# An opening in 128-token pieces, a first tile loaded by two queues, and GpSimd's setup moved behind the second set of loads

## The chip, the cores and the metric

The kernel runs on one core of a Trainium2 chip. The metric is device time in microseconds (us) of one launch, from many executions; each is listed with the clock that the throttle granted to TensorE. The profiled span is about 1.8 us shorter than the time of the same execution, so spans are compared with spans and times with times. Engine names: PE is TensorE, DVE is VectorE, ACT is ScalarE, POOL is GpSimd, SP is SyncE.

## The reference

Two layers of the same kind over 2048 tokens of width 1024 in bf16. Each layer has a dilated local attention (8 keys, 2 apart) and a token-mixing MLP (3584 wide).

```python
def _A_ref(x, wqkv, wo):                       # attention, 32 heads of 32
    qkv = (x @ wqkv).reshape(B, S, 3, H, Dh) ...
    idx = pos[:, None] - (arange(8) * 2)[None, :]       # keys s, s-2, ..., s-14
    logits = einsum("bhsd,bhswd->bhsw", q, k[idx]) * scale;  logits[idx < 0] = -1e9
    return einsum("bhsw,bhswd->bhsd", softmax(logits), v[idx]) ... @ wo
def _B_ref(x, w1, b1, w2, b2):                 # MLP over the tokens
    h = layernorm(x); u = gelu(einsum("bsd,sf->bdf", h, w1) + b1)
    return (einsum("bdf,fs->bds", u, w2) + b2).transpose(0, 2, 1)
x = A_x                                        # twice:
x = x + _A_ref(layernorm(x), wqkv, wo);  x = x + _B_ref(layernorm(x), w1, b1, w2, b2)
```

Since keys are 2 apart, even and odd tokens never meet in the attention. The kernel calls them class 0 and class 1 and works on 8 tiles of 128 tokens of each.

## The kernel before

Its opening loads the 8 tiles of class 0, normalizes and transposes them on the fly, and projects q, k and v. The tiles of class 1 are loaded into the same buffers as these come free, all eight by GpSimd's queue in order:

```python
def staged(c, i):
    n = (i + c * (NT - 1)) % NT          # class-1 tile 0 -> buffer 7, tile 1 -> buffer 0, ...
    return g[n // GF][:, n % GF, :]

def x_stage(c, i):
    eng = nc.gpsimd if c else (nc.scalar if i % 2 else nc.sync)
    eng.dma_start(out=staged(c, i), in_=xin_v[c, i])
# ... in first_tiles (8 tiles of class 0):
idle(16); moments(0); own_sum(0); moments(1); norm(0); turn(0); idle(3)
own_sum(1); moments(2); norm(1); turn(1); idle(5); place(0, act); ...
for u, i in (((1, 0), 2), ((1, 1), 3), ((0, 0), None)):      # first projections, 256 columns
    banks[u] = bank(); project(*u, 0, banks[u], 0, 2 * P)
# ... (cut)
for u in ((1, 0), (1, 1), (0, 0), (0, 1)):                   # the "second half"
    project(*u, 1, bank(), 0, HT)
# ... opening():
for i in range(NT): x_stage(0, i)
load_biases()
first_tiles(hT, partial(at_.project, 0))
for i in range(NT): x_stage(1, i)
```

`moments` are layer-norm statistics on DVE (BATCH_NORM_STATS2) with the root on ACT, `norm` normalizes, `turn` transposes on TensorE, `place` copies the transpose out of PSUM, `idle` are dummy products that keep TensorE clocked up. Class-1 tiles are handled by two engines in turn, and scores are a DVE product `T` that TensorE then sums over the head:

```python
def prologue_tile(c, i, hT):              # class 1
    t = staged(c, i)
    if i % 2: nm, rs = stats_act(t, ...);  norm_act(t, t, nm, rs)      # odd tiles on ACT
    else:     mean, rs = stats_dve(t, ...); norm_dve(t, t, mean, rs)   # even tiles on DVE
    to_hT(t, hT, c, i)                    # DMA transpose
# scores, for each pair of heads' group and parity:
T = q (broadcast) * window(k)             # DVE, 128x4096
sc += sel^T @ T                           # TensorE, 8 products of 512 columns; needs T
```

`sel` and `maskc` are constants that GpSimd writes with some forty small fills. q and k reach DVE through casts on ACT, which stand in ACT's program order between the statistics of class-1 tiles 1, 3, 5 and 7.

Of the kernel before, what the change touches and what calls it, by code (L numbers as in the profile page):

```python
# [15 lines left out]
P = 128  # L16
H = 32
DH = 32
# [4 lines left out]
NEG = -1e9  # L23
# [3 lines left out]
def kernel(  # L27
# [13 lines left out]
    nc = tc.nc  # L41
# [7 lines left out]
    NT = SC // P  # L49
    HT = SC // 2  # L50
    NDC = D // 512
    HD = P // DH
    DQ = 4
# [56 lines left out]
    def bank(name="ps"):  # L110
        return psp.tile([P, 512], FP32, name=name, tag="ps")
# [10 lines left out]
    def st(name, shape):  # L122
        return stat.tile(shape, FP32, name=name, tag=name)
# [13 lines left out]
    slots = wins[0] + wins[1]  # L137

    sel = const.tile([P, SB * DQ, 32], BF16, name="sel")
    nc.gpsimd.memset(sel[:], 0.0)  # L140
    for sb in range(SB):
        for dq in range(DQ):
            for hp in range(HD):
                col = sb * CH + dq * HD + hp
                nc.gpsimd.memset(sel[hp * DH:(hp + 1) * DH, sb * DQ + dq, col:col + 1], 1.0)
    maskc = const.tile([P, W, W], FP32, name="maskc")
    nc.gpsimd.memset(maskc[0:CH], 0.0)
    for s, w in enumerate(slots):
        if w:
            nc.gpsimd.memset(maskc[0:CH, s, 0:w], NEG)  # L150
    b1_bf = const.tile([P, FT], BF16, name="b1_bf")
    b2_bf = const.tile([P, NT, DIL], BF16, name="b2_bf")
    b1_sb = const.tile([P, FT], FP32, name="b1_sb")
    b2_sb = const.tile([P, NT, DIL], FP32, name="b2_sb")

    def load_biases():
        with nc.allow_non_contiguous_dma(reason="tiny bias loads"):
# [39 lines left out]
    def rsqrt(dst, var, mul, eps):  # L197

        ln = st("ln", [P, 1])
        nc.scalar.activation(out=ln[:], in_=var, func=ACT.Ln, bias=eps[:], scale=mul)  # L200
        nc.scalar.activation(out=dst, in_=ln[:], func=ACT.Exp, scale=-0.5)
# [33 lines left out]
    def norm_act(dst, x, nm, rs):  # L235
        bi = st("bi", [P, 1])
        nc.scalar.activation(out=bi[:], in_=nm[:], func=ACT.Identity, scale=rs[:])
        nc.scalar.activation(out=dst, in_=x, func=ACT.Identity, bias=bi[:], scale=rs[:])  # L238
# [4 lines left out]
    def staged(c, i):  # L243
        n = (i + c * (NT - 1)) % NT
        return g[n // GF][:, n % GF, :]

    def x_stage(c, i):
        eng = nc.gpsimd if c else (nc.scalar if i % 2 else nc.sync)
        eng.dma_start(out=staged(c, i), in_=xin_v[c, i])

    def first_tiles(hT, project):
        tiles = [staged(0, i) for i in range(NT)]
        mv, rs, tps = {}, {}, {}
        s1, t1, nm, ss = (st(n, [P, w]) for n, w in (("s1", NDC), ("t1", 1), ("nm", 1), ("ss", 1)))
        junk = x2("junk")
        own = NT // 2

        def idle(n):
            ps = bank()
            for _ in range(n):  # L260
                nc.tensor.matmul(ps[:].rearrange("p (b t) -> p b t", t=P), lhsT=ident[:],
                                 rhs=ident[:].unsqueeze(1).to_broadcast([P, 4, P]), start=True, stop=True)

        def moments(i):
            s = st("bn", [P, NDC, 6])
            for n in range(NDC):
                nc.vector.bn_stats(out=s[:, n, :], in_=tiles[i][:, n * 512:(n + 1) * 512])
            mv[i] = st("mv", [P, 2])
            nc.vector.bn_aggr(out=mv[i][:], in_=s[:])
            rs[i] = st("rs", [P, 1])  # L270
            rsqrt(rs[i][:], mv[i][:, 1:2], 1.0, eps1)

        def norm(i):
            norm_dve(tiles[i], tiles[i], mv[i][:, 0:1], rs[i])

        def own_sum(n):
            nc.scalar.activation(out=junk[:, n * 512:(n + 1) * 512], in_=tiles[own][:, n * 512:(n + 1) * 512],
                                 func=ACT.Identity, accum_out=s1[:, n:n + 1])

        def own_square():  # L280
            nc.scalar.activation(out=t1[:], in_=s1[:, 1:2], func=ACT.Copy, scale=-1.0 / D)
            nc.scalar.activation(out=nm[:], in_=s1[:, 0:1], func=ACT.Identity, bias=t1[:], scale=-1.0 / D)
            nc.scalar.activation(out=junk[:], in_=tiles[own], func=ACT.Square, bias=nm[:], accum_out=ss[:])
            rs[own] = st("rs", [P, 1])
            rsqrt(rs[own][:], ss[:], 1.0 / D, eps1)

        def turn(i):
            tps[i] = psp.tile([P, KD, P], BF16, name="tp", tag="ps")
            for kt in range(KD):
                nc.tensor.transpose(tps[i][:, kt, :], tiles[i][:, kt * P:(kt + 1) * P], ident[:])  # L290

        def place(i, copy):
            copy(out=hT[0][i // 4][:, :, (i % 4) * P:(i % 4 + 1) * P], in_=tps.pop(i)[:])

        dve, act = nc.vector.tensor_copy, nc.scalar.copy
        idle(16)
        moments(0)
        own_sum(0)
        moments(1)
        norm(0)  # L300
        turn(0)
        idle(3)
        own_sum(1)
        moments(2)
        norm(1)
        turn(1)
        idle(5)
        place(0, act)
        moments(3)
        place(1, dve)  # L310
        norm(2)
        norm(3)
        banks = {}
        for u, i in (((1, 0), 2), ((1, 1), 3), ((0, 0), None)):
            banks[u] = bank()
            project(*u, 0, banks[u], 0, 2 * P)
            if i:
                turn(i)
        own_square()
        place(2, act)  # L320
        place(3, dve)
        norm_act(tiles[own], tiles[own], nm, rs[own])
        moments(own + 1)
        moments(own + 2)
        for n, u in enumerate(banks):
            project(*u, 0, banks[u], 2 * P, HT)
            if n == 0:
                turn(own)
                norm(own + 1)
                place(own, dve)  # L330
                moments(own + 3)
                norm(own + 2)
        for n, u in enumerate(((0, 1), (1, 2), (1, 3))):
            if n == 2:
                norm(own + 3)
            turn(own + 1 + n)
            place(own + 1 + n, dve)
            project(*u, 0, bank(), 0, HT)
        for u in ((1, 0), (1, 1), (0, 0), (0, 1)):
            project(*u, 1, bank(), 0, HT)  # L340

# [519 lines left out]
    for li in range(2):  # L861
# [7 lines left out]
                nc.gpsimd.memset(t[:, :, 0:PADK + 2], 0.0)  # L869

        def opening():
            for i in range(NT):
                x_stage(0, i)
            load_biases()
            clear_pads()
            with tc.manual_schedule(engines={getattr(mybir.EngineType, e) for e in ("PE", "DVE", "Activation", "Pool")}):
                first_tiles(hT, partial(at_.project, 0))
                for i in range(NT):
                    x_stage(1, i)
            yield "at", 27.0, 29.0  # L880
            for u in ((1, 2, 1), (1, 3, 1), (0, 2, 0),):
                yield from at_.proj(0, *u)
# [75 lines left out]
```

## Time and profile before

| before | |
|---|---|
| time, median of 3 runs at first, of 6 beside the changed kernel | 1280.26 us; 1280.51 us (1280.16 to 1280.95) |
| profiled span, granted clock | 1278.8 us, 1.00 |
| first statistics, first projection, second half | 4.63, 11.98, 25.61 us |
| class-1 loads issued by GpSimd | 24.35 to 28.64 us |
| first T on DVE; waits of TensorE before the first two score products | 35.05 us; 0 and 1.24 us |

The lines that carry the reading are in the prediction. One more view: DVE's timeline between the opening and the first T (start, length, engine, line, operation, output and inputs, count, and in brackets the idle time before it and what ended that; line numbers are those of the kernel that ran).

```profile
27.47 1.29 DVE L207 BATCH_NORM_STATS2 bn<-gg 128x6 f32<-128x512 bf16 x2 [2.69 <-DMA gg<-in_A_x_dram]
30.34 1.29 DVE L207 BATCH_NORM_STATS2 bn<-gg 128x6 f32<-128x512 bf16 x2 [1.34 <-DMA gg<-in_A_x_dram]
32.13 1.28 DVE L207 BATCH_NORM_STATS2 bn<-gg 128x6 f32<-128x512 bf16 x2 [0.26 <-DMA gg<-in_A_x_dram]
33.34 0.53 DVE L233 TENSOR_SCALAR gg<-gg,mv,rs 128x1024 bf16<-128x1024 bf16 x1
```

DVE waits for class-1 tiles 0, 2 and 4 one after the other as they land, and reaches T 2.92 us after the last of these (35.05 - 32.13).

### The profile page before, as it was taken

The numbers are of one execution on the slowest core, as the hardware profiler recorded it, in microseconds if no ns is written. First come the engines' busy times: TensorE is split into PE (matmuls) and PEld (weight loads), VectorE is DVE, ScalarE is ACT, GpSimd is POOL, SyncE is SP. The second block draws the span as 40 slices with busy tenths as digits, with TensorE's granted clock in tenths as the row PEclk, the third lists the DMA queues.
The fourth block names the chain that finished last, engine by engine and source line by source line (L and its number), as shares of the span: only waits on it lengthen the run. The fifth ranks groups of instructions, "written<-read, shape, count | busy, mean of one in ns | idle before, by whom it ended". The sixth has DMA issues, their size and how long they took to land.

```text
span 1278.8 us, 15455 instructions
## 1 busy us (share of the span) xinstructions
PE 1258.0 (98%) x6163; PEld 577.4 (45%) x6284; DVE 689.9 (54%) x869; ACT 489.3 (38%) x812; POOL 61.3 (5%) x166
## 2 busy tenths in 40 slices
PE   8999999999999999999999999999999999999998
PEld 4344444444444444444444444444444444444444
DVE  6789999999114322334798834899930233111011
ACT  6845446634424533324533445453352343000000
POOL 3000000001000000000000000010010000000000
PEclk9999999999999999999999999999999999999999
DMA  9853454553422289952738542358262223344331
GB/s 256 190 124 106 99 139 142 171 143 115 132 83 83 64 220 305 291 161 87 187 103 201 152 124 80 83 159 207 66 181 83 82 67 89 107 128 135 99 115 52
DMA packets 217817, 173.00 MB, mean 135 GB/s; under 512 B 32081, under 2 KB 198353, under 8 KB 215697
## 3 DMA queue, kind: packets, MB, share of 16 engines
q1 hardware_dynamic: 206768, 126.11, 36.5%
q0 software_dynamic: 9248, 37.51, 10.5%
q10 hardware_dynamic: 1728, 8.39, 1.7%
q8 instruction: 49, 0.80, 0.3%
q14 instruction: 24, 0.19, 0.0%
HBM read 139.47 MB, written 26.21 MB: 130 GB/s over the span
## 4 chain that ended last, share of the span: by engine, by line
PE 76%; DVE 5%; issue 2%; ACT 1%; DMA 0%; DVEq 0%
PE ps L719 30%; PE ps L743 29%; PE ps L418 11%; PE ps L664 4%; DVE T L456 2%; PE sc L480 1%; DVE pr L538 1%; DVE pr L543 1%; DVE xr L689 0%; ACT h L227 0%; ACT h L238 0%; DMA wo<-in_A_wo_dram 0%; DVE v L545 0%; DVE xr L692 0%; ACT ln L200 0%
## 5 line engine op out<-in xcount | busy, mean ns | idle before, releaser
L719 PE MATMUL ps<-h,w 128*128 128x512 bf16 x1754 | 385.6, 379 | 4.0 <-ACT h L238 2.0
L743 PEld LDWEIGHTS <-w 128*128 128x128 bf16 x1820 | 177.6, 98 | 209.9 <-issue 2.1
L719 PEld LDWEIGHTS <-w 128*128 128x128 bf16 x1792 | 175.2, 98 | 214.1 <-issue 3.4
L418 PE MATMUL ps<-hT,wq 128*128 128x512 bf16 (+1 forms) x1087 | 240.2, 374 | 2.5 <-issue 0.6
L743 PE MATMUL ps<-g,w 128*128 128x512 bf16 (+1 forms) x1017 | 225.9, 376 | 1.2 <-issue 0.2
L743 PE MATMUL ps<-gg,w 128*128 128x512 bf16 (+1 forms) x766 | 170.9, 376 | 0.9 <-issue 0.2
L418 PEld LDWEIGHTS <-wq 128*128 128x128 bf16 x1112 | 109.1, 100 | 128.8 <-issue 9.1
L748 DVE SCALAR_TENSOR_TENSOR xr<-ps,b_sb,xr 128x512 bf16<-128x512 f32 (+1 forms) x65 | 45.5, 738 | 225.1 <-PE ps L743 182.6
L456 DVE TENSOR_TENSOR T<-q,k 128x4096 bf16<-128x4096 bf16 x44 | 99.0, 2284 | 70.5 <-ACT q L422 52.4
L543 DVE TENSOR_TENSOR pr<-pr 128x2048 bf16<-128x2048 bf16 (+1 forms) x128 | 119.4, 949 | 0.3
L730 DVE TENSOR_TENSOR tmp<-ps,gg 128x512 f32<-128x512 f32 x48 | 33.2, 692 | 150.2 <-PE ps L719 148.2
L418 PE MATMUL ps<-hT,wv 128*128 128x512 bf16 x436 | 99.5, 380 | 0.6
L664 PE MATMUL ps<-wo,oT 128*128 128x512 bf16 x377 | 88.6, 379 | 1.1 <-DVE oT L545 0.7
L425 ACT CAST k<-ps 128x1024 bf16<-128x1024 f32 x60 | 60.7, 1014 | 61.0 <-PE ps L418 59.0
L538 DVE TENSOR_TENSOR pr<-pb,v 128x2048 bf16<-128x2048 bf16 x64 | 75.9, 1218 | 10.8 <-ACT v L425 6.1
L538 DVE TENSOR_TENSOR pr<-pb,g 128x2048 bf16<-128x2048 bf16 x64 | 76.6, 1216 | 7.6 <-DMA pb<-pd 5.1
L418 PEld LDWEIGHTS <-wv 128*128 128x128 bf16 x448 | 48.9, 111 | 48.7 <-issue 4.2
L730 DVE TENSOR_TENSOR tmp<-ps,g 128x512 f32<-128x512 f32 x48 | 33.2, 692 | 49.7 <-PE ps L719 46.9
L664 PEld LDWEIGHTS <-oT 128*128 128x128 bf16 x384 | 37.3, 98 | 46.8 <-issue 1.2
L422 ACT CAST q<-ps 128x512 bf16<-128x512 f32 x60 | 34.9, 586 | 49.5 <-PE ps L418 49.5
L731 ACT ACTIVATE gg<-tmp,b_sb 128x512 bf16<-128x512 f32 x48 | 34.6, 721 | 49.9 <-DVE tmp L730 49.9
L731 ACT ACTIVATE g<-tmp,b_sb 128x512 bf16<-128x512 f32 x48 | 34.6, 721 | 43.5 <-DVE tmp L730 43.1
(97 smaller groups left out, 755.9 us busy)
## 6 DMA issues: line engine op xcount, KB each, us to landing
w<-in_B_w_dram SPq DMA_DIRECT2D x56, 512.0 KB, 4.8
w<-in_B_w_dram SPq DMA_DIRECT2D x64, 448.0 KB, 3.8
wq<-in_A_wqkv_dram SPq DMA_DIRECT2D x38, 512.0 KB, 4.3
pb<-pd POOLq DMA_DIRECT2D x16, 1024.0 KB, 8.7
wo<-in_A_wo_dram SPq DMA_DIRECT2D x16, 512.0 KB, 3.9
xa<-xr POOLq DMA_DIRECT2D x32, 256.0 KB, 3.4
xr<-xa SPq DMA_DIRECT2D x32, 256.0 KB, 4.0
wv<-in_A_wqkv_dram SPq DMA_DIRECT2D x14, 512.0 KB, 5.4
```

The costliest lines, as they stand in the source:

```text
L418: nc.tensor.matmul(ps[:, lo:hi], lhsT=cols, rhs=self.hT[c][hf][:, kt, lo:hi], start=(kt == 0), stop=(kt == KD - 1))
L422: nc.scalar.copy(out=self.q_of(c, dt)[:, hf * HT:(hf + 1) * HT], in_=ps[:])
L425: nc.scalar.copy(out=window(buf, 0, PADK + hf * HT, [(KW + 1, 2), (1, HT)]), in_=ps[:].unsqueeze(1).to_broadcast([P, 2, HT]))
L456: mult = nc.vector.tensor_tensor(out=T, in0=q.unsqueeze(1).to_broadcast([P, 4, SC]), in1=window(k, par, 2, [(2, 4), (1, SC)]), op=ALU.mult)
L538: mult = nc.vector.tensor_tensor(out=pr[:, :, u, :], in0=pb[:, :, u, :], in1=window(self.v_of(c, dt), par, 2 + hf * HT, [(TB, 4), (2, 4), ...
L543: nc.vector.tensor_tensor(out=pr[:, :, 0:wd, :], in0=pr[:, :, 0:wd, :], in1=pr[:, :, wd:2 * wd, :], op=ALU.add)
L664: nc.tensor.matmul(banks[(i, n)][:], lhsT=at_.oT[c][kt][:, i * P:(i + 1) * P], rhs=wo_t[n][kt // 4][:, kt % 4, :], start=(kt == 0), stop=( ...
L719: nc.tensor.matmul(ps[:], lhsT=wt[c][:, i, fl * P:(fl + 1) * P], rhs=h2[c][i // 4][:, i % 4, dc * 512:(dc + 1) * 512], start=(k == 0), sto ...
L730: nc.vector.tensor_tensor(out=tmp[:], in0=ps[:], in1=gs, op=ALU.add)
L731: nc.scalar.activation(out=gs, in_=tmp[:], func=ACT.Gelu_apprx_tanh, bias=b1_sb[:, ft:ft + 1])
L743: nc.tensor.matmul(ps[:, 0:xc.stop - xc.start], lhsT=w2t(ft, c), rhs=g[ft // GF][:, ft % GF, xc], start=(ft == 0), stop=(ft == FT - 1))
L748: nc.vector.scalar_tensor_tensor(out=xo[:, xc], in0=ps[:, 0:xc.stop - xc.start], scalar=b2_sb[:, i, c:c + 1], in1=xo[:, xc], op0=ALU.add, ...
```

## The change

The intent: put the first tile at the head of both queues, interleave statistics so that tile 0 is normalized sooner, start projecting with 128 columns as soon as one tile is transposed, and clear GpSimd's queue and the DMA engines of setup work in the first microseconds.

```diff
+    def constants():                      # sel and maskc: formerly at the start, as straight code
+        nc.gpsimd.memset(sel[:], 0.0); ...
-        idle(16); moments(0); own_sum(0); moments(1); norm(0); turn(0); ...
+        idle(14)
+        stats(0, 0); stats(0, 1); root(0); stats(1, 0); norm(0); turn(0); stats(1, 1); root(1)
+        place(0, act); own_sum(0); idle(3); stats(2, 0); norm(1); turn(1)
+        for u in ((1, 0), (1, 1)):
+            project(*u, 0, banks[u], 0, P)             # 128 columns
         ... (order of the other tiles cut; second half unchanged)
         def opening():
-            for i in range(NT): x_stage(0, i)
-            load_biases()
+            x_stage(nc.sync, 0, 0, slice(0, P // 2))
+            x_stage(nc.scalar, 0, 0, slice(P // 2, P))
+            x_stage(nc.scalar, 0, 1)
+            x_stage(nc.sync, 0, 2); at_.weights(0, 1, 0); x_stage(nc.scalar, 0, 3); ...
             first_tiles(...)
             for i in range(NT):
                 x_stage(nc.gpsimd, 1, i)
+            constants()
+            load_biases()
```

## The prediction

> **What bounds the kernel now.** I read the page first, then busy time by stretch, then the timeline of the first 50 us. The page says that TensorE is busy for nearly the whole span:
>
> ```profile
> span 1278.8 us, 15455 instructions
> PE 1258.0 (98%) x6163; PEld 577.4 (45%) x6284; DVE 689.9 (54%) x869; ACT 489.3 (38%) x812; POOL 61.3 (5%) x166
> ```
>
> So 20.8 us of TensorE idle time (1278.8 - 1258.0) is all there is to win, besides work that counts as busy and is not needed. The stretches (start:end, length, then busy us of PE, PEld, DVE, ACT, POOL, then clock, DMA share, GB/s) tell where it lies:
>
> ```profile
> 0.00:12.00 12.00, 8.28 (x41) 3.46 (x42) 7.32 (x18) 5.52 (x16) 7.57 (x61) 1.00 0.92 265
> 12.00:25.60 13.60, 13.45 (x119) 9.38 (x121) 9.46 (x19) 9.63 (x19) 1.65 (x5) 1.00 1.09 230
> 25.60:32.60 7.00, 6.95 (x33) 3.21 (x33) 3.46 (x7) 5.15 (x13) 3.04 (x6) 1.00 0.94 299
> 32.60:40.00 7.40, 6.16 (x41) 2.51 (x39) 7.40 (x11) 7.40 (x21) 0.00 (x0) 1.00 0.83 184
> ```
>
> From 12 us on TensorE is full, with one hole in the fourth row. Before 12 us it is idle for 3.7 us, and most of its 8.28 busy us is the dummy products (16 + 3 + 5) that only keep it clocked up. The timeline shows what ends this phase (start, length, engine, line, operation):
>
> ```profile
> 1.57 5.30 PE L261 MATMUL ps<-ident 128*128 128x512 bf16 x16 [1.57 <-POOL ident masks.py:199]
> 4.63 1.29 DVE L267 BATCH_NORM_STATS2 bn<-gg 128x6 f32<-128x512 bf16 x2 [3.73 <-DMA gg<-in_A_x_dram]
> 7.47 0.54 DVE L233 TENSOR_SCALAR gg<-gg,mv,rs 128x1024 bf16<-128x1024 bf16 x1
> 8.06 0.62 PE L290 MATMUL tp<-ident,gg 128*128 128x128 bf16 x8 [1.19 <-DVE gg L233]
> 9.35 0.49 DVE L233 TENSOR_SCALAR gg<-gg,mv,rs 128x1024 bf16<-128x1024 bf16 x1
> 11.20 0.64 DVE L293 COPY hT<-tp 128x1024 bf16<-128x1024 bf16 x1
> 11.98 1.03 PE L418 MATMUL ps<-hT,wq 128*128 128x256 bf16 x8 [0.38 <-ACT t L281]
> 25.61 7.07 PE L418 MATMUL ps<-hT,wq 128*128 128x512 bf16 x31
> ```
>
> Tile 0 lands at 4.63, is normalized at 7.47, transposed at 8.06; the first projection has 256 columns, so it needs tiles 0 and 1, and starts at 11.98, just after the copy of tile 1 ends (11.20 + 0.64 = 11.84). The named releaser, a small ACT instruction, is a coincidence: the program has no such dependence. From 11.98 TensorE runs without a break to the second half (25.61) and to 32.6. **The opening is a chain load, statistics, root, normalize, transpose, copy, and the rest of the kernel is TensorE work behind it.**
>
> **What the Trainium skill says.** "DMA: Bandwidth & Descriptors", Rules for kernel authors: splitting a transfer into partition halves, or over SP and ACT, buys no bandwidth, since both share the same 16 DMA engines. The trace agrees: tiles 0 and 1, issued at 0.74 (SP) and 0.77 (ACT), landed 3.9 and 4.0 us later, together. So the split of tile 0 can help only by putting it alone at the head of both queues. The same section: a strided last dimension becomes one descriptor per element. The bias loads are such (3,584 + 2,048 two-byte elements); between 12 and 16 us, before they land, the DMA engines are mostly busy yet move 77 GB/s on average, against 335 to 385 from 4 to 10 us. "TensorE: Matmul & The Clock Gate", part 1: the array starts at half clock and needs some 3.4 us of activity; the weight loads of the dummies are 0.43 us apart up to 4.96 and 0.2 after, so the clock is up by about 5 us.
>
> **The change, part by part.** Writing t0 for the landing of tile 0, with durations from the timeline.
>
> *Loads.* The bytes moved by 3.9 us (sum of the GB/s slices) are about 0.51 MB, the size of two tiles, and both had landed 0.7 us later. Alone at the head, 0.26 MB is moved by about 3.15; adding the same 0.7 gives t0 = 3.85, a gain of 0.8 us (estimate). Key weights went fifth on SP (issued 2.61, landed 10.9); now they go third, behind about 1.3 MB in all, so they land near 7 (estimate), well before they are needed. Tiles 5 to 7 move back to about 9.5 to 11 and are needed from 12.
>
> *DVE order.* Before, all of tile 1's statistics stood between tile 0's and its normalization (start to start 7.47 - 4.63 = 2.84). Now only one half does: two halves of 0.64, aggregate 0.13, half of tile 1 under ACT's two root steps (0.77 from the aggregate's start), gives 2.12. Gain 0.7 us.
>
> *Pieces.* Following all engines in program order from t0: tile 0 normalized 2.12, transposed 2.7; its copy on ACT stands behind the root of tile 1 and runs 3.9 to 4.9; tile 1 normalized 4.0, transposed 4.6 to 5.2. The first 128-column products start at t0 + 5.2 = 9.0, not 11.98. They add little: eight transposes, of the same width, step through in 0.45 us, so two pieces cost 0.9 as does the 256-column group (0.9 to 0.95 by its spacing). Then, from t0: two pieces to 6.1; wait for tile 2's transpose, 6.5; two second pieces to 7.85; query group 8.8; transpose 9.2; second query group 10.1; four 256-column groups with two transposes to 14.7; a 512-column group (1.72) 16.4; transpose, 256 columns, transpose, 256 columns to 19.1. ACT is close behind (the tile it normalizes itself is ready at 12.4, wanted at 12.9), and the last copy (19.0) just precedes the second half. **The second half starts at t0 + 19.1 = 22.95, not 25.61: 2.66 us earlier**, of which 0.8 from the load and the rest from order and pieces. Seven dummies fewer cost nothing: they filled waits.
>
> *GpSimd.* The identity comes no later: six pad fills take the place of the large fill of 0.32 us. Its constants (about 5 us) now follow the class-1 loads. Those wait for the last transpose, so they move from 24.35 to about 22.4 and are issued by 26.7; constants end near 32. Their first reader, the score product, was at 37.80 and will come near 35: 3 us to spare. The bias loads then meet the class-1 transposes and cost DMA a slow stretch like that of 12 to 16 us, but near 32 to 37. Biases themselves are not read for hundreds of us.
>
> *What follows.* Products after the second half run on without waits to the first score product. The hole there is its second half, waiting for DVE:
>
> ```profile
> 35.05 2.27 DVE L456 TENSOR_TENSOR T<-q,k 128x4096 bf16<-128x4096 bf16 x1
> 39.65 0.61 PE L480 MATMUL sc<-T,sel 128*32 128x512 bf16 x8 [1.24 <-DVE T L456]
> ```
>
> DVE came to it late because class-1 tiles landed late (idle until 27.5, 30.3, 32.1). They now have DMA nearly to themselves, so I expect DVE near 31.7 instead of 35.05, and the hole to shrink from 1.24 to about 0.7. Sum: 2.66 + 0.5 = 3.2 us at 40 us. I take off 0.5 for parts of the later schedule that DVE sets (95.1 of 100 us busy from 100 to 200) and for DMA delays: **2.7 us, 1277.6 us, 0.2%.**
>
> **Rivals.** (a) *Nothing is gained*: the attention stage has DVE at 95%, so a head start on TensorE is given back as waits for DVE. Against: TensorE idles only 1.2 of 100 us there, and DVE starts earlier too. It would leave 1280. (b) *The bias loads hurt*: in 40 to 60 us the DMA share is 0.98, so a slow stretch of about 4 us at 33 delays class-1 transposes and weights. For: those transposes (issued 33.9 to 55) are in its way. Against: class-1 rows are first multiplied near 70, last transposed near 60, and weights then due were issued 10 us ahead. It would give back 1 to 2 us: 1278.5 to 1279.5. (c) *Small pieces or a lower clock*: if waits between pieces let the clock fall, some 3.4 us at half speed would cost 1.7 us or more; the kernel before has a gap of 1.19 us at 8 without that, so I think it unlikely. (d) *A better load*: if tile 0 lands by 3.3, the gain is 3.3 or more: 1276.5 or so.
>
> **Range and chances.** One class of outcome, a head start of 1 to 4 us, carries nearly all the weight. The low end, 1276.2, is (d) with the whole of the hole gone; the high end, 1279.6, is (b) in full. Two per cent is 25.6 us, more than all idle time of TensorE, so faster by 2% is out of reach; slower by 2% would need a new wait of 26 us, which no part can make. Before's three runs span 0.16 us, so the noise is small.
>
> **What would show it.** Right: first DVE statistics near 3.85; first projection near 9.0; second half near 22.95; class-1 loads issued near 22.4; PE busy in the first 12 us more useful, no new hole before 60, and total PE idle near 19.5 (seven dummies, some 1.7 us, are gone as well). The load step is wrong if statistics still begin near 4.6. Rival (b) shows as PE waits on DMA or later class-1 transposes; (a) as larger PE waits for DVE between 60 and 320; (c) as 128-column groups well over 0.45 us or dummies slow again. The prediction fails if the second half starts early and the end does not follow.

## The result, and the profile after

The changed kernel takes 1284.7 us (median of 6 runs, 1282.17 to 1287.32), the kernel before 1280.51 us (1280.16 to 1280.95) in the same rounds. The ratio is 1.0031, 95% interval 1.0017 to 1.0044. Ratios here and below are the mean time of one kernel's runs over that of the other's of the same rounds, so not quite the ratio of the medians quoted. The time lies above the predicted range (1276.2 to 1279.6) and on the other side of the kernel before.

The runs do not agree with each other as those of the kernel before do. Two with a mean granted clock of 1.0 took 1282.17 and 1282.53 us; the four with 0.999 or 0.997 took 1284.33 to 1287.32. So about 1.8 us is lost even at full clock (1282.35 - 1280.51), and more comes with a lower clock.

The opening, in the order of the lines that the prediction showed (two of DVE's statistics, DVE's normalization, the first projection, the second half):

```profile
4.19 1.29 DVE L268 BATCH_NORM_STATS2 bn<-gg 128x6 f32<-128x512 bf16 x2 [3.29 <-DMA gg<-in_A_x_dram]
6.65 0.69 DVE L268 BATCH_NORM_STATS2 bn<-gg 128x6 f32<-128x512 bf16 x1 [0.94 <-DMA gg<-in_A_x_dram]
7.26 0.53 DVE L235 TENSOR_SCALAR gg<-gg,mv,rs 128x1024 bf16<-128x1024 bf16 x1
...
10.30 1.06 PE L444 MATMUL ps<-hT,wq 128*128 128x128 bf16 x16
24.28 7.08 PE L444 MATMUL ps<-hT,wq 128*128 128x512 bf16 x32
```

The second half starts 1.33 us earlier (25.61 - 24.28), half of the 2.66 predicted. The second line says where the rest is: tile 0 landed at 4.19, but half of tile 1's statistics, next on DVE, waited until 6.65 for the load of tile 1. In the kernel before both tiles had landed by 4.8.

Then the stretches, with the same columns as in the prediction (start:end, length, busy us of PE, PEld, DVE, ACT, POOL, then clock, DMA share, GB/s). First two of the changed kernel, then the second of them in the kernel before (its first is in the prediction):

```profile
32.60:40.00 7.40, 4.55 (x27) 1.86 (x25) 6.65 (x9) 7.34 (x19) 3.03 (x12) 1.00 0.69 89
40.00:50.00 10.00, 8.50 (x48) 2.78 (x48) 7.33 (x6) 10.00 (x31) 1.16 (x2) 0.83 1.18 232
```

```profile
40.00:50.00 10.00, 9.89 (x61) 4.02 (x56) 5.95 (x6) 10.00 (x30) 0.00 (x0) 1.00 0.96 201
```

Between 32.6 and 40 us TensorE is busy for 4.55 us where it was for 6.16, and in the next stretch its clock is 0.83. The timelines of DVE, ACT and TensorE say why:

```profile
26.74 1.29 DVE L209 BATCH_NORM_STATS2 bn<-gg 128x6 f32<-128x512 bf16 x2 [2.52 <-DMA gg<-in_A_x_dram]
29.56 1.29 DVE L209 BATCH_NORM_STATS2 bn<-gg 128x6 f32<-128x512 bf16 x2 [1.29 <-DMA gg<-in_A_x_dram]
33.35 0.69 DVE L209 BATCH_NORM_STATS2 bn<-gg 128x6 f32<-128x512 bf16 x1 [2.27 <-DMA gg<-in_A_x_dram]
33.96 1.16 DVE L235 TENSOR_SCALAR gg<-gg,mv,rs 128x1024 bf16<-128x1024 bf16 x1
36.90 2.27 DVE L482 TENSOR_TENSOR T<-q,k 128x4096 bf16<-128x4096 bf16 x1
...
32.66 0.63 ACT L222 ACTIVATE junk<-gg 128x512 bf16<-128x512 bf16 x1 [1.74 <-DMA gg<-in_A_x_dram]
...
39.22 0.61 PE L506 MATMUL sc<-T,sel 128*32 128x512 bf16 x8 [2.68 <-DVE T L482]
41.50 1.02 PE L506 MATMUL sc<-T,sel 128*32 128x512 bf16 x8 [1.66 <-DVE T L482]
42.45 3.35 PE L444 MATMUL ps<-hT,wv 128*128 128x512 bf16 x9
```

DVE again waits for class-1 tiles 0, 2 and 4, but the last comes at 33.35, 1.22 us later than before, and the normalization after it takes 1.16 us instead of 0.53. Together that is the 1.85 us by which the first T is late (36.90 against 35.05). ACT waits too, for tile 3, until 32.66. TensorE, ahead by 1.33 us, now waits 2.68 us for the first T and 1.66 us for the second. The score products in between are only 0.61 us of work. After that its products run slowly: nine of 512 columns take 3.35 us, 0.37 us each, against 2.11 us for nine in the kernel before. At full clock they would have taken some 2 us; with the slow second score product (1.02 instead of 0.61), that one spell costs about 1.7 us. Late T (1.85) and slow clock (1.7) add up to 3.6 of the 3.7 us by which the spans differ (1282.5 - 1278.8). This sum is arithmetic on two traces; the experiments have to show that the parts belong together.

The fifth score product tells where the loss is made. It starts at 51.85 us in the kernel before and at 56.10 in the changed one, 4.25 us late, and the spans differ by 3.7. In seven of the runs below (e1, e3, e4, e11, e12, e14, e18) its delay agrees with the difference of the spans to 0.6 us; e2 and e8 lose 1.4 and 0.8 us more after it. So nearly all of the loss is there by 56 us.

The slow normalization (0.63 of the 1.85 us) falls into the time in which GpSimd issues the first bias load, 33.31 to 34.89 us, so this part may belong to the moved GpSimd work. There is one more such case, 1.56 us at 7.31 in e6, again during that issue (6.91 to 8.64). But normalizations that overlap it in the kernel before (7.47) and in e8 (32.99) took 0.54 and 0.53. No run tests this.

(The busy total of TensorE on the page is of no use here. It says 1265.8 us after and 1258.0 before, but the older trace shows 6163 products and 6284 weight loads: some records are missing in it. So the prediction's 20.8 us of idle time, and the 19.5 that it expected after the change, cannot be checked by it.)

### The profile page after: what moved, and what is told of

It is laid out like the page before. It is cut to its first block, busy times and chain, and to the rows that moved or that the text cites. A ratio compares the mean times of both kernels' runs of the same rounds, so it can differ in the third digit from the quotient of the medians.

```text
span 1282.5 us, 15630 instructions
## 1 busy us (share of the span) xinstructions
PE 1265.8 (99%) x6309; PEld 578.6 (45%) x6309; DVE 691.2 (54%) x869; ACT 489.4 (38%) x812; POOL 61.9 (5%) x166
## 4 chain that ended last, share of the span: by engine, by line
PE 76%; DVE 5%; issue 2%; ACT 1%; DMA 0%; DVEq 0%
PE ps L745 30%; PE ps L769 29%; PE ps L444 11%; PE ps L690 4%; DVE T L482 2%; PE sc L506 1%; DVE pr L564 1%; DVE pr L569 1%; DVE xr L715 0%; ACT h L229 0%; ACT h L240 0%; DMA hT<-hb 0%; DVE v L571 0%; DVE xr L718 0%; ACT ln L202 0%
## 5 line engine op out<-in xcount | busy, mean ns | idle before, releaser
L444 PE MATMUL ps<-hT,wq 128*128 128x512 bf16 (+2 forms) x1136 | 241.7, 371 | 0.5 <-DMA hT<-hb 0.3
L444 PE MATMUL ps<-hT,wv 128*128 128x512 bf16 (+1 forms) x456 | 101.8, 379 | 0.0
```

Of the source, the lines that this page charges most:

```text
L444: nc.tensor.matmul(ps[:, lo:hi], lhsT=cols, rhs=self.hT[c][hf][:, kt, lo:hi], start=(kt == 0), stop=(kt == KD - 1))
```

## The experiments

The main theory (R in the later expectations) was that T does not come earlier because it hangs on the class-1 loads and on ACT and DVE behind them, so that the head start is only waited away, and that the waits then cost clock. Rivals: the moved GpSimd work (constants or biases) does the harm; or the order of work on DVE and ACT does; or one weight load collides with the class-1 loads (theory Q). Eighteen kernels were run, all with correct results. "T" is the start of the first T, "waits" are those of TensorE before the first two score products.

| run | built on | median us (runs) | ratio to before, 95% | second half | T | waits | clock 40-50 us |
|---|---|---|---|---|---|---|---|
| before | | 1280.51 (6) | | 25.61 | 35.05 | 1.24 | 1.00 |
| after | | 1284.7 (6) | 1.0031 [1.0017, 1.0044] | 24.28 | 36.90 | 4.34 | 0.83 |
| e1_const_early | after | 1283.14 (5) | 1.0020 [1.0008, 1.0033] | 25.00 | 36.02 | 2.75 | 0.83 |
| e2_bias_early | after | 1288.73 (6) | 1.0060 [1.0046, 1.0073] | 30.39 | 41.09 | 2.43 | 1.00 |
| e3_both_early | after | 1284.21 (6) | 1.0033 [1.0017, 1.0049] | 26.78 | 37.45 | 2.41 | 0.83 |
| e4_before_late | before | 1280.28 (5) | 0.9997 [0.9985, 1.0009] | 25.52 | 34.85 | 1.14 | 1.00 |
| e8_dummies | after | 1282.33 (4) | 1.0022 [1.0007, 1.0036] | 23.90 | 35.30 | 1.03 | 1.00 |
| e11_t_ahead | after | 1281.55 (4) | 1.0008 [0.9994, 1.0023] | 25.09 | 32.30 | 0 | 1.00 |
| e12_before_t_ahead | before | 1281.53 (4) | 1.0007 [0.9994, 1.0020] | 25.62 | 32.81 | 0 | 1.00 |
| e6_class1_sp | after | 1295.4 (4) | 1.0122 [1.0108, 1.0137] | 40.50 | 48.35 | 0 | 1.00 |
| e14_wq_held | after | 1285.61 (4) | 1.0039 [1.0024, 1.0055] | 24.69 | 35.95 | 2.99 | 0.83 |
| e15_load_order | after | 1281.71 (4) | 1.0011 [0.9996, 1.0025] | 26.14 | 35.10 | 0.76 | 1.00 |
| e16_before_load_order | before | 1287.5 (4) | 1.0054 [1.0039, 1.0069] | 34.61 | 41.50 | 0 | 1.00 |
| e18_no_split | after | 1282.02 (4) | 1.0010 [0.9993, 1.0026] | 23.84 | 34.20 | 2.09 | 0.87 |
| e21_order6 | after | 1281.38 (4) | 1.0007 [0.9992, 1.0022] | 24.72 | 36.67 | 3.17 | 1.00 |
| e19_whole_order6 | after | 1281.07 (5) | 1.0011 [0.9998, 1.0023] | 23.77 | 35.28 | 2.72 | 1.00 |
| e20_whole_order7 | after | 1283.44 (5) | 1.0023 [1.0011, 1.0036] | 23.82 | 38.38 | 3.55 | 0.83 |
| e22_whole_order6_t | after | 1281.94 (4) | 1.0012 [0.9999, 1.0026] | 23.76 | 32.57 | 0.53 | 0.83 |
| e23_whole_placed | after | 1281.21 (5) | 1.0003 [0.9989, 1.0017] | 23.83 | 32.42 | 0.79 | 1.00 |
| e24_before_late_placed | before | 1281.17 (5) | 1.0004 [0.9992, 1.0017] | 25.54 | 34.17 | 0.39 | 1.00 |

The last four columns are from one profiled execution each; times and ratios rest on all runs. A change in such a kernel also makes the scheduler move some instructions elsewhere, so differences of a few tenths are not read. The clock column is not complete either: over the first 12 us of the kernel before it reads 1.00, although the weight loads of the dummies are 0.43 us apart there until 4.96 us and 0.2 after.

### The moved GpSimd work

Four runs took it back, in part or whole, or gave it to the kernel before.

```diff
 e1: +    constants()                      # at the start again, biases stay late
     -                constants()
 e2: +            load_biases()            # ahead of the opening again, constants stay late
     -                load_biases()
 e3: both of these
 e4: the kernel before, with constants() and load_biases() behind the class-1 loads
```

> The changed kernel with only the constant fills back at the start; the bias loads stay behind the class-1 loads. Theory P (GpSimd work behind the class-1 loads makes tiles 3 and 4 of class 1 land late, so the first T starts at 36.90 instead of 35.05): if it is the fills, tile 4 lands by 32 and the first T starts near 35 or sooner, time 1279 to 1280.5. If it is the bias loads, which now come right behind the loads at 28, T stays at 36 to 37 and the time at 1282 to 1285. Theory Q (the head start itself, with the next weight load issued at 27.9 instead of 29.3, takes the DMA from the class-1 tiles): no change, 1282 to 1285.

> The changed kernel with only the bias loads back at the start, the constant fills stay behind the class-1 loads. Theory P with the fills as culprit: no change, first T near 36.9, 1282 to 1285. Theory P with the bias loads as culprit: T near 35 or sooner, 1279 to 1280.5. Theory Q: no change in T, 1282 to 1285. The slow DMA stretch of two-byte elements should be back near 12 to 16.

> The changed kernel with both back at the start, so only the pieces, the order and the loads of the opening are changed. Theory P: the first T starts at 35 or sooner, second half still near 24.3, time 1278.5 to 1280.5. Theory Q: T near 36.9, 1282 to 1285. If the head start of 1.3 us reached the end in full: 1279.2.

> The kernel before with only the constants and the bias loads moved behind the class-1 loads. Theory P: second half at 25.6 as before, first T near 37, time 1282 to 1285. Theory Q: first T at 35 as before, time 1280 to 1280.6.

Measured: moving the work late is worth nothing to the kernel before (e4, 0.9997). Taking only the constants back does not turn the loss into a gain (e1: waits of 1.09 and 1.66 us, clock 0.83, still slower than before). Taking the biases back makes the new opening worse. In e2 the bias loads, two bytes an element, then meet the opening's own loads: DMA moves only 149, 52, 67 and 102 GB/s in the four microseconds from 8 to 12, TensorE waits until 13.31 for the first query weights, and the second half starts at 30.39 us instead of 24.28. With both back (e3) it starts at 26.78, and the time is 1284.21 us, no better than with both late. So the new opening needs the late biases, and late GpSimd work does not explain the loss: alone it costs nothing (e4), its first bias load goes out at 33.31 us in the changed kernel, when tile 4 is just landing (33.35), and e23 below has it late too and loses nothing clear of noise. Only the 0.63 us of the slow normalization stay open.

### The clock by itself

e8 puts ten dummy products (of the identity, as in the opening) in front of the first score product of the changed kernel, so that TensorE is not idle while it waits.

```diff
+            keep_clock(10)                # 10 matmuls ident x ident, 512 columns, result unused
```

> The changed kernel with 10 dummy products (2.2 us at full clock) ahead of the first score product, in the gap of 2.68 us; nothing else. Theory C (part of the loss, and all of its scatter, is the TensorE clock that falls after the two gaps): clock 1.0 from 40 to 50, all runs within 1 us of each other near 1282.3, which is before plus the 1.85 us by which the second T is late. If the clock does not matter: 1284 to 1285 with the same scatter of 5 us.

Measured: the clock stays 1.00 from 40 to 50 us, though TensorE still waits 1.03 us at the second score product:

```profile
39.89 0.62 PE L506 MATMUL sc<-T,sel 128*32 128x512 bf16 x8 [1.03 <-DVE T L482]
```

Three of four runs are at 1282.24 to 1282.39 us, just where the two full-clock runs of the changed kernel are (1282.17 and 1282.53); the fourth took 1285.7 us, also at a mean clock of 1.0, for a reason not found. All four have a mean clock of 1.0, against two of six of the changed kernel. The low clock is thus a consequence of the idle time, and most of the step from 1282.3 to 1284.7 us goes with it. How much time it costs is less sure: the ratios of the two kernels overlap (1.0022 [1.0007, 1.0036] against 1.0031 [1.0017, 1.0044]), and in e20 and e22 below the one run at a clock of 1.0 (1283.44 and 1281.88 us) lies among those at 0.998 and 0.999 (1282.87 to 1283.82 and 1281.5 to 1282.54). The dummies do not win back the first 1.8 us. In this profile the first T is late by 0.25 us only (35.30), and TensorE waits for later ones: 0.48 us at 45.70 and 1.43 at 52.81.

### The order of work on DVE and ACT

e11 puts the first two T, and the cast of q that they need, ahead of the statistics of class-1 tiles 3 to 7 in the program order of DVE and ACT. e12 does the same to the kernel before.

```diff
+            b = nc.vector.bn_stats(...)
+            if after is not None: follow(b, after, NoSync)       # after the first two T
 stats_act likewise (after the q cast);  qk(0, 0) is issued before the class-1 tiles
```

> The changed kernel with one thing more: the first two T products (and the query copy they need) stand ahead of the statistics of class-1 tiles 3 and later in the DVE and ACT programs, so that no load of those tiles can hold them up. Theory R (in-order engines: the first T waits on DVE behind class-1 statistics that wait for late tiles, and TensorE waits for T, so the head start is lost in that wait): first T near 32 instead of 36.9, no wait of TensorE before the score products, clock 1.0 from 40 to 50, and the whole head start arrives: 1280.5 - 1.3 (second half earlier) - 1.2 (the hole of the kernel before) = 1278.0. Rival S (the 128-column pieces and the new order slow something later, or DVE is the bound later): T early, but the time stays at 1281 or more.

> The kernel before with the same reordering of T ahead of the class-1 statistics, opening otherwise untouched. Theory R: the hole of 1.24 us goes, T starts near 33 to 33.5, time 1279.2; so the change on top of it is then worth 1.2 us (the first run of this batch less this one). Rival S: 1280.5 (DVE time lost later), or faster than the first run of this batch.

Measured: T starts at 32.30 us (32.81 in e12), and TensorE runs through both score products without a wait. The wait has only moved: 1.57 us before the third score product in e11 and 1.56 us in e12.

```profile
32.30 4.49 DVE L488 TENSOR_TENSOR T<-q,k 128x4096 bf16<-128x4096 bf16 x2
...
41.94 0.61 PE L512 MATMUL sc<-T,sel 128*32 128x512 bf16 x8 [1.57 <-DVE T L488]
```

Both expected times (1278.0 and 1279.2 us) were missed. Against the kernel before, e12 loses about 1 us in the medians, not clear of noise. This suggests that the amount of work on ACT and DVE in this stretch counts, more than its order; ACT is busy for 10.00 of 10 us from 40 to 50 us in both kernels. In the profiled execution of e11 the clock stays up, and the changed kernel in this order is within 0.08% of the kernel before (one of its four runs had 0.997 and took 1283.49 us).

### Who delays the class-1 tiles

e6 moves the class-1 loads to SP's queue; e14 holds back the one weight load (512 KB, query weights) that SP issued at 27.93 us, amid the class-1 loads.

```diff
 e6:  -                    x_stage(nc.gpsimd, 1, i)
      +                    x_stage(nc.sync, 1, i)
 e14: +                    if self.li == 0 and key == (0, 0, 2): follow(d, self.first_t, Sync)
```

> The changed kernel with the class-1 tiles loaded by SP's queue instead of GpSimd's. Each can then be issued as its own buffer comes free (from about 17 on), not all behind the last transpose. Theory R: tile 4 lands before 30, the first T starts at 32 to 33, no wait of TensorE, 1278 to 1279. If the DMA is full with weights until 22 and the tiles only trade places with them: tile 4 near 31, 1279 to 1281. Rival S: T early, time 1281 or more.

> The changed kernel, with one thing held back: the query-weight load (512 KB) that its SP queue issued at 27.93 us, among the eight class-1 loads, now follows the first score operand (T) on DVE. Theory Q (that load delays the class-1 loads): tiles 3 and 4 of class 1 land near 30.5 to 31.5 us, not 32.6 and 33.2; ACT does not wait 1.74 us for tile 3; first T near 35, not 36.90; clock 1.0 in 40 to 50 us; about 1280.5 us. Rival (order of issue, landing and release has nothing to do with the weights): tiles 3 and 4 land at 32.5 to 33.5 as before, T at 36.5 to 37, and 1283 to 1285 us. The weights themselves could come late: then the products behind them wait on DMA between 40 and 50 us.

e6 was a miss, and it does not test the queue as such, since two more things moved with the edit. GpSimd, with no class-1 loads in front, did its setup at the start again and issued the bias loads from 6.91 us, into the opening as in e2. And the order of instructions changed: the sums of class-1 tiles came to stand in front of the statistics of a class-0 tile in ACT's program. ACT then stood still for a tile that SP issued at 19.44 us or later, and TensorE behind it:

```profile
25.38 0.63 ACT L222 ACTIVATE junk<-gg 128x512 bf16<-128x512 bf16 x1 [10.52 <-DMA gg<-in_A_x_dram]
...
32.45 1.03 PE L299 MATMUL tp<-ident,gg 128*128 128x128 bf16 x8 [13.05 <-ACT gg L240]
```

It does show how strictly these engines keep their order. The Trainium skill says so ("Perfetto Trace Analysis", Tensor Engine Instruction: ACT, DVE and GpSimd "are strict FIFO"), and here it costs 13.05 us.

e14 speaks against the collision with the weights, though its tile 3 and its T (35.95) came between the values expected by the two theories. With the load held until 38.29 us, tile 3 is there at 31.73, 7.5 us after the first class-1 issue; in e18, with the load at 27.50 us, it comes 7.3 us after; in the changed kernel 8.9 us after. So in these three traces the landing varies by more than the weight load can account for. e14 has waits of 1.33 and 1.66 us, a clock of 0.83, and 1285.61 us.

### Loads freed earlier

GpSimd issues the class-1 loads in order, and tile 0 goes into buffer 7, which is freed by the last transpose of the opening. So all eight stand behind that, and the DMA engines have nothing to do. Here are the GB/s in 40 slices of 1 us from 0 to 40 us, first of the changed kernel:

```profile
GB/s 0 0 223 279 260 290 348 357 327 303 358 377 322 292 291 290 290 315 335 349 349 290 56 6 0 225 307 201 238 287 295 361 356 269 87 20 16 10 57 65
```

and then of the kernel before:

```profile
GB/s 0 37 188 303 369 385 371 340 346 335 301 210 21 78 60 150 276 282 288 292 312 339 351 346 298 110 330 299 197 307 320 356 347 315 109 138 123 61 211 263
```

From 22 to 25 us the changed kernel moves 56, 6 and 0 GB/s, while the kernel before was still catching up on what its bias loads had held up from 12 to 16 us. The opening's loads got out of the way earlier, and nothing took the place. e15 and e16 reorder the issue so that tile 0 is last (in the changed kernel and in the one before); the loads then start at 14.82 us in e15 and 17.61 in e16.

```diff
-                for i in range(NT):
+                for i in (4, 1, 2, 3, 5, 6, 7, 0):       # e15, e16
+                for i in (6, 1, 2, 3, 4, 5, 7, 0):       # e21, e19, e22: from about 20 us
+                for i in (7, 1, 2, 3, 4, 5, 6, 0):       # e20: from about 22 us
```

> The changed kernel, with GpSimd issuing the eight class-1 loads in the order 4, 1, 2, 3, 5, 6, 7, 0: tile 0 goes into the buffer that is freed last, and in front of the others on an in-order queue it holds all of them until 23.8 us. Theory R (the stretch from 24 to 60 us is a chain class-1 load, statistics, T, softmax): most class-1 tiles are issued from about 15 us on and landed by 27, ACT and DVE do not wait for them between 28 and 34 us, the first T comes at 33 to 34.5 (36.90 before), T from g near 48.5 to 49.5 (51.42), the clock stays 1.0 in 40 to 50, and the time is 1278 to 1280 us. Rival (the new opening itself costs time later, or the clock falls for another reason): 1283 us or more with the tiles early.

> The kernel before, with the same order of the class-1 loads (4, 1, 2, 3, 5, 6, 7, 0) and nothing else. Theory R: class-1 tiles land before 28 us instead of 27.5 to 34.2, ACT's wait of 1.58 us for tile 1 goes, T from g starts 0.5 to 1.5 us before 49.51, and the time is 1279 to 1280 us. If the head start of TensorE counts after all, the changed kernel with this order is 1 to 1.5 us faster than this one; if only the chain counts, the two are within 0.7 us. Risk: early class-1 loads get into the way of x tiles 5 to 7 and of the weights, and the second half starts later than 25.61.

Too early: e15 has tiles 1 to 5 by about 25 us (tile 0, now last, at 29.2) and its T<-g (the first score operands of the next heads) at 47.06 instead of 51.42, but the loads take DMA time from the opening. TensorE loses 1.86 us to a late class-0 tile, and 2.75 us to late value weights far behind. e16 loses 6.59 us to a class-0 tile, as its opening is later.

```profile
24.74 0.62 PE L299 MATMUL tp<-ident,gg 128*128 128x128 bf16 x8 [1.86 <-DVE gg L235]
132.49 7.96 PE L444 MATMUL ps<-hT,wv 128*128 128x512 bf16 x35 [2.75 <-DMA wv<-in_A_wqkv_dram]
```

The next runs start the loads at about 20 or 22 us, when the opening's loads are through, and three of them also load tile 0 whole again.

> The changed kernel, with the class-1 loads issued in the order 6, 1, 2, 3, 4, 5, 7, 0, so that seven of eight are freed by the transpose of class-0 tile 5 (about 20.1 us) and not by the last (23.8). The weights of the opening have then all but landed, unlike in e15_load_order. Theory R (the loads' lateness makes T late): loads run in the DMA gap from 22 to 25 us, class-1 tiles land by 29, the second score product waits under 1.3 us, the clock is 1.0 in 40 to 50, no wait of TensorE for wv, and the time is 1280.5 to 1282 us. Rival (T is late by the order of work on ACT and DVE): first T at 36 or later, waits of 2.5 us or more before the score products, 1283 to 1285 us.

> Tile 0 whole and the loads in the order 6, 1, 2, 3, 4, 5, 7, 0. Theory R: second half near 23.9, first T at 32.5 to 33.5 us, PE waits before the score products at most 1.3 us in all, clock 1.0 throughout, 1278.5 to 1280 us: faster than both kernels. Rival (order of work on ACT and DVE): 1281.5 to 1283 us, as e18_no_split.

> As e19_whole_order6, but in the order 7, 1, 2, 3, 4, 5, 6, 0, so that the loads start about 22.3 us, after all loads of the opening. If weights or x tiles were held up in e19_whole_order6, this one is the faster; if only the start of the class-1 loads counts, it stands between e18_no_split and e19_whole_order6: 1279.5 to 1281.5 us, first T near 33.5.

> e19_whole_order6 with the first two T and the query copy placed ahead of the statistics of class-1 tiles 3 to 7 (as in e11_t_ahead). If ACT and DVE are no longer short of work and T comes in time in e19_whole_order6, this changes nothing or loses up to 1 us by moving the wait behind the score products (as e12_before_t_ahead did to the kernel before); if the order still binds, it gains 1 us against e19_whole_order6.

e21 came out between the theories: T at 36.67 us and waits of 3.17, as its rival expected, but a clock of 1.00 and 1281.38 us, as theory R did. So a long wait is not always followed by a low clock or a long time. The pair e19 and e20 differs in nothing but the time at which the loads are freed, 19.80 and 22.02 us (and what the scheduler makes of it). The first T comes at 35.28 and 38.38 us, the waits are 2.72 and 3.55 us, the clock is 1.00 and 0.83, the time 1281.07 and 1283.44 us. That fits the chain of the theory up to the clock: load, T, wait, clock. The step to the time is not shown by it: these are medians, their ratios overlap, and the two profiled executions took 1284.71 (e19) and 1283.03 us (e20). The expected T near 33 us did not come, though, since tile 0 is first on DVE and was now loaded last:

```profile
29.85 1.88 DVE L209 BATCH_NORM_STATS2 bn<-gg 128x6 f32<-128x512 bf16 x3 [6.13 <-DMA gg<-in_A_x_dram]
...
37.60 0.61 PE L506 MATMUL sc<-T,sel 128*32 128x512 bf16 x8 [1.57 <-DVE T L482]
40.34 0.61 PE L506 MATMUL sc<-T,sel 128*32 128x512 bf16 x8 [1.15 <-DVE T L482]
...
131.17 9.65 PE L444 MATMUL ps<-hT,wv 128*128 128x512 bf16 x36 [2.34 <-DMA wv<-in_A_wqkv_dram]
```

DVE stood 6.13 us for it with the other tiles in place. The last line is again a late load of value weights, 2.34 us at 131 us; the loads that broadcast the attention probabilities, 1 MB each on GpSimd's queue, took 12.3 us to land there, against 9.1 us in the kernel before, and the value weights 9.2 us against 4.9. That was the execution of 1284.71 us; the other four of e19 took 1279.84 to 1282.75.

e22, with T ahead, moves the wait again, to the third score product, and the clock is 0.83 there; at 1281.94 us it is 0.9 us above e19, within the noise:

```profile
42.73 1.05 PE L512 MATMUL sc<-T,sel 128*32 128x512 bf16 x8 [2.53 <-DVE T L488]
```

### The split of tile 0

```diff
-            x_stage(nc.sync, 0, 0, slice(0, P // 2))
-            x_stage(nc.scalar, 0, 0, slice(P // 2, P))
+            x_stage(nc.sync, 0, 0)
             x_stage(nc.scalar, 0, 1)
```

> The changed kernel with x tile 0 loaded whole on SP and tile 1 whole on ACT, as in the kernel before; order and pieces as in the changed kernel. If the split bought what the changed trace shows (first statistics 4.63 to 4.19), statistics begin near 4.6 here, tile 1 is there with it (no wait until 6.65 for its second half), and the second half starts within 0.3 us of 24.28: a gain on tile 0 that tile 1 gives back. If the split is worth its 0.44 us to the end of the opening, the second half starts near 24.7. The total then stays at 1283 to 1286 us in either case.

Measured: statistics start at 4.69 us, later than with the split, but tile 1 is there and tile 0 is normalized at 6.82 us, against 7.26.

```profile
4.69 1.29 DVE L268 BATCH_NORM_STATS2 bn<-gg 128x6 f32<-128x512 bf16 x2 [3.80 <-DMA gg<-in_A_x_dram]
...
36.53 0.62 PE L506 MATMUL sc<-T,sel 128*32 128x512 bf16 x8 [0.43 <-DVE T L482]
38.81 0.67 PE L506 MATMUL sc<-T,sel 128*32 128x512 bf16 x8 [1.66 <-DVE T L482]
```

In the five profiles with tile 0 whole (e18, e19, e20, e22, e23), statistics start at 4.61 to 4.69 us, tile 0 is normalized at 6.74 to 6.82 and the second half starts at 23.76 to 23.84. In seven with the split and the biases late (after, e1, e8, e11, e14, e15, e21), statistics start at 4.19 to 4.96 us, tile 0 is normalized at 6.35 to 8.08, and the second half (without e15, whose early loads disturb it) starts at 23.90 to 25.09. So the split starts the first tile up to 0.5 us sooner, and mostly gives back more on the second: a loss on average, and the source of the opening's scatter. Time 1282.02 us, 1.0010, less than the 1283 to 1286 expected. TensorE is 1.77 us ahead of the kernel before here, and T 0.85 us; the difference is again waited away, in 0.43 and 1.66 us, with a clock of 0.87.

### All of it together

e23 loads tile 0 whole and puts the class-1 tiles into other buffers, so that tile 0 can be loaded first, at 19.86 us. e24 does the same to the kernel before with its GpSimd work late (e4), so that the two differ by the opening alone.

```diff
-        n = (i + c * (NT - 1)) % NT
+        n = (5, 0, 1, 2, 3, 4, 6, 7)[i] if c else i
+        (statistics of class-1 tile 0 kept behind the opening's last copy on DVE)
```

> The changed kernel with x tile 0 loaded whole and the class-1 tiles put into other buffers (tile 0 into that of class-0 tile 5, tiles 1 to 5 into those of tiles 0 to 4), loads in natural order: all but the last two are freed at about 19.8 us, tile 0 first. Theory R: DVE has class-1 tile 0 by 23.5 us and does not wait later; first T at 32 to 33.5 us; PE waits before the score products at most 1.3 us; clock 1.0; 1278.3 to 1280 us, under both kernels. Rival (order of work on ACT sets T): first T at 34 or later, 1281 to 1282.5 us as e18_no_split, e19_whole_order6.

> e4_before_late with the class-1 tiles in the same other buffers as in e23_whole_placed: loads freed before 22 us. TensorE has no head start here, so with T early it does not wait at all before the score products (1.1 in e4_before_late): theory R gives 1279 to 1280 us, that is 0.5 to 1 us above e23_whole_placed. If the two are equal, or this one is the faster, the new opening is worth nothing even with early loads.

```profile
24.35 2.10 DVE L211 BATCH_NORM_STATS2 bn<-gg 128x6 f32<-128x512 bf16 x3 [0.58 <-DMA gg<-in_A_x_dram]
27.90 0.69 DVE L211 BATCH_NORM_STATS2 bn<-gg 128x6 f32<-128x512 bf16 x1 [0.79 <-DMA gg<-in_A_x_dram]
32.42 2.29 DVE L486 TENSOR_TENSOR T<-q,k 128x4096 bf16<-128x4096 bf16 x1 [0.98 <-ACT q L452]
...
37.43 0.62 PE L510 MATMUL sc<-T,sel 128*32 128x512 bf16 x8 [0.79 <-DVE T L486]
43.25 0.61 PE L510 MATMUL sc<-T,sel 128*32 128x512 bf16 x8 [0.57 <-DVE T L486]
49.33 0.62 PE L510 MATMUL sc<-T,sel 128*32 128x512 bf16 x8 [1.26 <-DVE T L486]
```

Theory R is confirmed in the middle and refuted at the end. DVE has tile 0 at 24.35 us and waits for no tile after 27.90, T starts at 32.42 instead of 36.90, no wait is longer than 1.3 us, the clock is 1.0 in all five runs. The time is 1281.21 us, 1.0003: not below the kernel before. e24, without the new opening, takes 1281.17 us. So with early loads the two openings cannot be told apart, although one has TensorE at the second half 1.7 us sooner (23.83 against 25.54); each interval is about 1.8 us wide to either side, so part of that could still be there. The first T now waits for a cast on ACT (0.98 us in the third line), and ACT is busy for 14.96 of 15 us from 25 to 40 us and 10.00 of 10 from 40 to 50: the bound seems to have moved there, and TensorE waits in three small pieces (0.79, 0.57, 1.26 us) for what comes behind it. No run made ACT's work lighter, so this is argued and not shown. The profiled execution of e23 has the shortest span of all (1277.9 against 1278.8 us), half of its head start kept; two of five runs took 1279.4 to 1279.7 us, three 1281.2 to 1282.0. A late load of value weights like those of e15 and e19 would explain the difference, but no trace of a slower e23 run was taken, so that stays open. No version was found that is surely faster than the kernel before.

## Why the prediction was wrong

**Bound.** Right. From 12 us on TensorE is the bound, and the time is its work plus its waits plus lost clock. What the prediction left out is the last term.

**Loads.** Mis-sized. First statistics at 3.85 predicted, 4.19 measured: a gain of 0.44 us, not 0.8. The cost was not seen at all: tile 1 stands behind half of tile 0 on ACT's queue and came nearly 2 us later than before.

**DVE order.** Right in its working, and spoiled by the load: 2.12 us from first statistics to normalization predicted, 3.07 measured (7.26 - 4.19). With tile 0 loaded whole it is 2.13 us (e18). That it hits the 2.12 so closely is partly luck: the terms listed give 2.05 (two halves of 0.64 and 0.77 from the aggregate's start), or 2.18 with the aggregate counted again.

**Pieces.** Right. From that normalization to the first projection 3.03 us were predicted (9.0 - 3.85 - 2.12) and 3.04 measured; from there to the second half 13.95 predicted and 13.98 measured. The 128-column pieces cost what they should (sixteen products in 1.06 us). Rival (c), small pieces or a lower clock in the opening, is refuted. So the head start was 1.33 us and not 2.66, and the whole shortfall is in the landing of tiles 0 and 1.

**GpSimd.** Right. The class-1 loads went out 0.5 us before the second half, as predicted (23.80; 22.4 was predicted with an earlier second half), and its constants came well before their first reader. Moved alone, this work changes nothing (e4). Not foreseen was the slow normalization beside the first bias load (0.63 us), which may belong here.

**What follows.** This is the step that failed: "They now have DMA nearly to themselves, so I expect DVE near 31.7 instead of 35.05, and the hole to shrink from 1.24 to about 0.7." T came at 36.90, and the hole grew to 4.34 us. A term of +0.5 us was -3.1 us. Two things were wrong in it. The loads were brought forward by 0.55 us only, since they stay behind the last transpose, and their landing then scatters by more than that. And the claim that a head start of TensorE reaches 40 us was never checked against what TensorE needs there: T, which hangs on class-1 loads, ACT and DVE. The prediction's own view had shown DVE waiting for those tiles; the right reading of it was that TensorE was already early before the change.

**Rivals.** (a), a head start that is given back as waits for DVE, is what happened, at 37 to 41 us and not between 60 and 320. It was put at 1280, because a wait was thought to cost no more than the head start. It can cost more when it is long: some 2.4 us of the result go with a lower clock (1284.7 - 1282.3). (b), the late bias loads, shows one of its two signs: the first class-1 transpose is issued at 35.15 us instead of 33.90 and lands in 6.5 us instead of 3.7. But TensorE does not wait for DMA in the changed kernel before 60 us, and in e4 the first four transposes take 6.3 us (median) instead of 4.2 and nothing is lost. (d) did not occur.

**Range.** Its upper end, 1279.6, came from (b) alone, although (a) was put at 1280, outside it. With (a) and the clock in it, it would have had to reach beyond the kernel before. The chances for 2% were right.

Still open: why one execution's class-1 tiles land up to 1.5 us later than another's, and what splits the runs of e23 into two groups.

## What to carry to other kernels

Before you count a head start as a gain, name the next thing that the engine will wait for and ask whether that moves too; here it hung on loads in an in-order queue and on two other engines. A bound engine that is made to arrive earlier at an unmoved wait idles longer in one piece. Here the clock of TensorE fell after some of these pieces (0.83 after one of 3.55 us in e20, 1.00 after 2.02 and 1.15 in e21), so a change can lose more than it gains. Loading the first tile through two queues delayed here what stood behind it on the second queue: look at when the second tile lands, not only the first.

## What the Trainium skill lacked or had wrong

- "TensorE: Matmul & The Clock Gate", part 1 and the table of "Why this matters for your kernels": it warns of idle gaps of more than about 3 us, one window of some 3.4 us. Here single waits were shorter and the clock fell: 1.33 and 1.66 us with 0.61 us of score product between gave 0.83 over 40 to 50 us (e14), 0.43 and 1.66 gave 0.87 (e18). So a mostly idle stretch can be enough, though not always: 0.75 and 1.66 gave 0.83 (e3) and 0.77 and 1.66 gave 1.00 (e2). The page's "A second HAM failure mode" comes near to this, with short idles between groups of products that make the clock swing, but gives no lengths. The page says that the window runs freely, which fits such chance; no run here shows it directly.
- "DMA: Bandwidth & Descriptors", Anatomy of one DMA: its fit (2.0 us plus bytes over 436 GB/s) gives an estimate of 2.6 us for a 256 KB load from GpSimd. The first of eight landed in 3.1 us in the kernel before and 2.9 in the changed one; the median of the eight was 5.5 us in the kernel before, 7.2 in the changed one. For several loads in a row the page's figure is a floor only.
- The same page, Rules for kernel authors, says that splitting a transfer over SP and ACT buys no bandwidth. The opening gained nothing from it here, and the runs add what the page lacks: the next tile comes late and at a varying time. Tile 0 was normalized at 6.35 to 8.08 us with the split (seven profiles), at 6.74 to 6.82 without it (five).
